# A float64 rounding's last addition on VectorE, a folded matrix two roundings behind, and token sums apart from their read

## The chip, the cores and the metric

The kernel runs on one core of a Trainium2 chip. A core has five engines with a queue each, which run in order: TensorE (PE, matmuls into PSUM; PEld is its weight load), VectorE (DVE), ScalarE (ACT), GpSimd (POOL) and SyncE (SP, which here only issues transfers). ACT and POOL issue transfers too, between their other instructions. Instructions on different engines wait for each other through semaphores. The metric is the device time of one execution in microseconds (us).

## The reference

Eight sequences of 3008 tokens with 256 channels pass a filter in the frequency domain and then an MLP mixer. All tokens' data are float32, the mixer's weights are float64.

```python
X = np.fft.rfft(x, axis=1)
y = np.fft.irfft(X * (filt_r + 1j * filt_i)[None], n=3008, axis=1)   # (8, 3008, 256)
h = np.maximum(y.transpose(0, 2, 1) @ w_tok1, 0.0) @ w_tok2          # (3008, 256), (256, 3008)
u = y + h.transpose(0, 2, 1)
out = u + np.maximum(u @ w_ch1, 0.0) @ w_ch2                         # (256, 1536), (1536, 256)
```

## The kernel before

**The filter.** 3008 = 47 x 64, so the Fourier transform is made of matmuls with small matrices. For each sequence 12 units (`a_unit`) transform x over the 64 and write the result to `z_tmp` in DRAM; x is loaded by SP into three tiles used in turn, the load for unit i + 3 issued behind unit i. Then come 32 frequency steps. `b_unit` reads its rows of `z_tmp` back, transforms over the 47 (PE), and multiplies by the filter (four DVE instructions, lines 378 to 381); `bi_unit` transforms back over the 47 and writes to `g_tmp`. The filter is loaded for two steps at a time into three tiles used in turn; for the first sequence SP, ACT and POOL issue these loads, for the others SP alone. `dft(bs)` is a generator that yields between units and steps: 12 units, 2 empty yields, 33 steps for the first sequence.

**The inverse over the 64** is not made for itself. It is a matrix `wai`. For the tokens it is multiplied into `w_tok1` beforehand: `w1_fold(i)` (line 241) multiplies two of the 24 slices of `w1` by it on PE, into the PSUM bank `po0` or `po1`, and ACT copies the result over the slices (line 246).

**The weights** arrive as float64 and are rounded to float32 on the chip (`rounded`, line 203): POOL issues the load into a staging tile, ACT takes the top bits (line 217), four DVE instructions (218, 219, 221, 223) build a truncated number `top` and the `rest`, and POOL adds the two into the weight (line 225). `top` and `rest` of the early weights lie in one tile `both`, of which there are two. `weights()` yields after each rounding, and each call of `next(convert)` makes one and then issues the load six ahead. The order: 12 tiles of `w1`, 16 of `w2`, 2 of `wc1`, and 10 late ones of `wc1` and `wc2`, of which those of `wc2` are followed by five more POOL instructions (lines 289 to 293) that form sums for a fast matrix product.

**The order of the work** is written by hand: each engine's queue is in the order of the program. The first sequence's transform runs first, with the 12 roundings of `w1` between its units (every second) and its steps (every third, up to step 15), each followed at once by its fold. Then SP issues the loads of the result (`t4_load`), the 16 roundings of `w2` follow, then `token_hidden(0)`: the token matmuls (line 423) into the bank `acc` and the ReLU on ACT (line 426). Two roundings of `wc1` and the first mixer tiles (`u_unit`: lines 437, 442, 444) come next. From there `mix` runs over six token tiles of six hidden pairs for each sequence, with the ten late roundings in its first half items and the next sequences' transforms spread among its items. `hidden` (449, 451), `sums` (464 to 466) and `products` (480) form an item, and POOL issues the stores of the output.

Of the kernel before, what the change touches and what calls it, by code (L numbers as in the profile page):

```python
# [14 lines left out]
ALU = mybir.AluOpType  # L15
# [5 lines left out]
N2 = 64  # L21
# [4 lines left out]
A = 24  # L26
# [9 lines left out]
TC = DT // P  # L36
# [7 lines left out]
NG = 8  # L44
# [69 lines left out]
def kernel(  # L114
# [11 lines left out]
    nc = tc.nc  # L126
# [33 lines left out]
    def bank(tag):  # L160
        return (psg if tag == "pg" else psum).tile([P, 512], FP32, tag=tag, name="ps_" + tag)
# [41 lines left out]
    def rounded(st, n, parts, late=False):  # L203

        words = [st.bitcast(t).rearrange("p (n w) -> p n w", w=2)[:, 0:n] for t in (U32, FP32)]
        lo, hi, hi_f = words[0][:, :, 0], words[0][:, :, 1], words[1][:, :, 1]
        if late:

            top = pp.tile([P, 512], FP32, tag="p1", name="top")[:, 0:n]
            rest = pp.tile([P, 512], FP32, tag="p2", name="rest")[:, 0:n]  # L210
        else:
            both = hp.tile([P, 2, 512], FP32, tag="hh", name="both")
            top, rest = both[:, 0, 0:n], both[:, 1, 0:n]
        top_i, rest_i = top.bitcast(U32), rest.bitcast(U32)


        nc.scalar.activation(out=top, in_=hi_f, func=AF.Copy, scale=2.0 ** -112)  # L217
        nc.vector.tensor_scalar(out=top_i, in0=top_i, scalar1=3, scalar2=None, op0=ALU.logical_shift_left)
        nc.vector.scalar_tensor_tensor(out=top_i, in0=hi, scalar=0x80000000, in1=top_i,  # L219
                                       op0=ALU.bitwise_and, op1=ALU.bitwise_or)  # L220
        nc.vector.tensor_scalar(out=rest_i, in0=top_i, scalar1=0xFF800000, scalar2=None, op0=ALU.bitwise_and)  # L221

        nc.vector.scalar_tensor_tensor(out=rest, in0=lo, scalar=2.0 ** -52, in1=rest, op0=ALU.mult, op1=ALU.mult)  # L223
        for src, dst in parts:
            nc.gpsimd.tensor_tensor(out=dst, in0=src(top), in1=src(rest), op=ALU.add)  # L225

    def w1_load(i):
        st = stage(512)
# [12 lines left out]
    def w1_fold(i):  # L241

        ps = bank("po%d" % (i % 2))
        w = w1[:, 2 * i:2 * i + 2, :].rearrange("p a t -> p (a t)")
        nc.tensor.matmul(ps, wai_t, w, start=True, stop=True)
        nc.scalar.copy(out=w, in_=ps)
# [169 lines left out]
        t4[b, c] = t4p.tile([P, TC4, D], FP32, tag="t4", name="t4")  # L416
        nc.sync.dma_start(t4[b, c], rows_of(g_d, b)[:, ts(c, TC4), :])

    def token_hidden(b):
        acc = bank("acc").rearrange("p (t d) -> p t d", t=TC)  # L420
        for a in range(A):
            for t in range(TC):
                nc.tensor.matmul(acc[:, t, :], w1[:, a, ts(t, P)], t4[b, a // TC4][:, a % TC4, :],  # L423
                                 start=(a == 0 and t == 0), stop=(a == A - 1 and t == TC - 1))
        h1 = h1p.tile([P, TC, D], FP32, tag="h1", name="h1")
        nc.scalar.activation(out=h1, in_=acc, func=AF.Relu)  # L426
        return h1

    def width(m):
        return 512 if m < MT - 1 else 448  # L430
# [15 lines left out]
    def hidden(ut, jt, w, hh):  # L446
        ps = bank("pg")
        for c in range(DH):
            nc.tensor.matmul(ps[:, 0:w], wc1[:, c, ts(jt, P)], ut[:, c, 0:w],  # L449
                             start=(c == 0), stop=(c == DH - 1))  # L450
        nc.scalar.activation(out=hh[:, jt % 2, 0:w], in_=ps[:, 0:w], func=AF.Relu)  # L451
# [8 lines left out]
    def sums(hh, w):  # L460
        hw = w // 2
        t = tp.tile([P, 4, 256], FP32, tag="t", name="t")
        v = nc.vector.tensor_tensor
        v(out=t[:, 0:2, 0:hw], in0=hh[:, :, hw:w], in1=hh[:, 0, 0:w].rearrange("p (s n) -> p s n", s=2), op=ALU.subtract)  # L464
        v(out=t[:, 2, 0:hw], in0=t[:, 1, 0:hw], in1=hh[:, 0, 0:hw], op=ALU.add)  # L465
        v(out=t[:, 3, 0:hw], in0=t[:, 2, 0:hw], in1=hh[:, 1, 0:hw], op=ALU.subtract)  # L466
        return t

    def products(m, jp, hh, t, po):
        w = width(m)  # L470
        hw = w // 2
        if jp == 0:
            for i in range(4):
                po.append(bank("po%d" % i).rearrange("p (s n) -> p s n", s=2))
        b11, b21, b22 = hh[:, 0, 0:hw], hh[:, 1, 0:hw], hh[:, 1, hw:w]
        t1, t3, t2, t4_ = (t[:, i, 0:hw] for i in range(4))
        todo = ((1, b21), (2, b22)), ((3, t4_), (6, t1)), ((0, b11), (5, t2)), ((4, t3),)
        for i, parts in enumerate(todo):
            for j, (n, mov) in enumerate(parts):
                nc.tensor.matmul(po[i][:, j, 0:hw], wc2[:, jp, n, :], mov, start=(jp == 0 and j == 0),  # L480
                                 stop=(jp == JP - 1 and j == len(parts) - 1))
# [35 lines left out]
    h1s, uts = {}, {}  # L517

    def u_part(b, m, dh):
        if dh == 0:  # L520
            uts[b, m] = up.tile([P, DH, 512], FP32, tag="u", name="u")
        u_unit(b, m, h1s[b], uts[b, m], dh)

    def mix(b, next_ready, convert):

        wait = [0]
        pos, hhs, sms = {}, {}, {}
        more = b + 1 < B

        items = [(m, jp) for m in range(MT) for jp in range(JP)]  # L530
        n = len(items)
        for i in range(n + 1):
            for half in range(2):
                next(convert, None)
                if i < n:
                    m, jp = items[i]
                    if half == 0:
                        hhs[i] = hp.tile([P, 2, 512], FP32, tag="hh", name="hh")
                    hidden(uts[b, m], 2 * jp + half, width(m), hhs[i])
                    if half == 1:  # L540
                        sms[i] = sums(hhs[i], width(m))
                        if m + 1 < MT and jp in (2, 3):
                            u_part(b, m + 1, jp - 2)
                            if jp == 3:
                                wait.append(m + 1)
                        if more and i == n - 2:
                            h1s[b + 1] = token_hidden(b + 1)
                        if more and i == n - 1:
                            u_part(b + 1, 0, 0)
                elif more and half == 0:  # L550
                    u_part(b + 1, 0, 1)
                if half == 1 and i >= 1:
                    m, jp = items[i - 1]
                    products(m, jp, hhs.pop(i - 1), sms.pop(i - 1), pos.setdefault(m, []))
                    if jp == JP - 1:
                        finish(b, m, uts[b, m], pos[m])
                if more and next_ready():
                    for c in wait:
                        t4_load(b + 1, c)
                    wait.clear()  # L560
                yield

    with tc.manual_schedule():
        nc.sync.dma_start(wa, wa_d)
        nc.vector.memset(xlast[HALF:P, XC - 1, :], 0.0)
        for t in filts:
            nc.vector.memset(t, 0.0)
        convert = weights()
        next(convert)
        folds = iter(range(A // 2))  # L570
        for i, _ in enumerate(dft(GROUPS[0])):
            if i == 0:
                for t, src in ((wai_t, wait_d), (wai, wai_d)):
                    nc.scalar.dma_start(t, src)

            if i % 2 == 1 and i < NXC or i % 3 == 2 and NXC < i <= NXC + 3 * (A // 4):
                next(convert)
                w1_fold(next(folds))
        assert next(folds, None) is None
        for c in range(A // TC4):  # L580
            t4_load(0, c)
        for _ in range(TC * N2 // NG):
            next(convert)
        h1s[0] = token_hidden(0)
        for _ in range(DH):
            next(convert)
        for dh in range(DH):
            u_part(0, 0, dh)
        for bs, after in zip(GROUPS, GROUPS[1:] + ((),)):
            todo = dft(after) if after else iter(())  # L590
            done = not after
            for b in bs:
                def next_ready():
                    return b != bs[-1] or done

                for i, _ in enumerate(mix(b, next_ready, convert)):
                    if not done and i % len(bs) == 0:
                        done = next(todo, "end") == "end"
            for _ in todo:
                raise AssertionError("the filter's steps don't fit beside the mixer's")  # L600
# [30 lines left out]
```

## Time and profile before

| | |
|---|---|
| median of 3 runs | 2754.22 us (2753.38 to 2755.7) |
| the profiled execution | 2754.93 us, its span 2753.2 us |
| instructions | 26044 |
| PE busy | 2603.7 us, 95% of the span |
| DVE busy | 1214.5 us, 44% |
| ACT busy | 528.6 us, 19% |
| POOL busy | 558.1 us, 20% |

A row of the timeline has the start and the length in us, engine, line, operation, the tile written and those read, shapes, the number of instructions that it merges, and in brackets how long the engine had been idle and what ended that. `ACTq`, `SPq` are the queues' own instructions, among them the issues of transfers. In a table by stage each engine has its busy time and its instructions in brackets; the last three columns are PE's granted clock (1.00 is full), the mean busy share of the 16 DMA engines and the GB/s that they moved. A row of the waits names who waited for whom, the total, the times and the longest. In a table of groups stand the busy time, the mean length of one in ns, and the idle time before them. The view of transfers has packets, bytes and the mean rate.

### The profile page before, as it was taken

The numbers are of one execution on the slowest core, as the hardware profiler recorded it, in microseconds if no ns is written. First come the engines' busy times: TensorE is split into PE (matmuls) and PEld (weight loads), VectorE is DVE, ScalarE is ACT, GpSimd is POOL, SyncE is SP. The second block draws the span as 40 slices with busy tenths as digits, with TensorE's granted clock in tenths as the row PEclk, the third lists the DMA queues.
The fourth block names the chain that finished last, engine by engine and source line by source line (L and its number), as shares of the span: only waits on it lengthen the run. The fifth ranks groups of instructions, "written<-read, shape, count | busy, mean of one in ns | idle before, by whom it ended". The sixth has DMA issues, their size and how long they took to land.

```text
span 2753.2 us, 26044 instructions
## 1 busy us (share of the span) xinstructions
PE 2603.7 (95%) x9112; PEld 1677.2 (61%) x9112; DVE 1214.5 (44%) x2244; ACT 528.6 (19%) x941; POOL 558.1 (20%) x973
## 2 busy tenths in 40 slices
PE   4466999999999999999999999999999999999997
PEld 1234655576666665676666765676666766676665
DVE  2478557723235455423325455432345443323333
ACT  1112222212222122112221112111212111111111
POOL 2338411112112111211212111121121121212121
PEclk8668999999999999999999999999999999999999
DMA  6455444323232222212223222211322111000000
GB/s 173 134 180 163 130 129 119 92 79 102 73 103 73 63 82 68 73 27 68 84 90 87 73 75 81 71 35 53 96 62 75 53 45 48 23 8 15 8 16 15
DMA packets 166488, 209.40 MB, mean 76 GB/s; under 512 B 35740, under 2 KB 114993, under 8 KB 166358
## 3 DMA queue, kind: packets, MB, share of 16 engines
q1 hardware_dynamic: 92297, 111.04, 13.8%
q0 software_dynamic: 30976, 44.53, 6.4%
q10 hardware_dynamic: 43085, 52.17, 5.8%
q8 instruction: 73, 1.20, 0.2%
q14 instruction: 57, 0.47, 0.1%
HBM read 132.63 MB, written 74.97 MB: 75 GB/s over the span
## 4 chain that ended last, share of the span: by engine, by line
PE 90%; DVE 4%; issue 2%; DMA 2%; POOL 1%; ACT 0%; SPq 0%; ACTq 0%; DVEq 0%; POOLq 0%
PE ps_pg L449 35%; PE ps_po L480 31%; PE ps_acc L437 6%; PE ps_acc L423 5%; PE ps_acc L386 4%; PE ps_b L370 4%; PE ps_acc L442 3%; PE ps_b L338 2%; DVE both L219 1%; POOL w L225 1%; DMA filt<-in_filt_r_dram 1%; DVE both L223 0%; DMA filt<-in_filt_i_dram 0%; DMA x<-in_x_dram 0%; DVE both L221 0%
## 5 line engine op out<-in xcount | busy, mean ns | idle before, releaser
L449 PE MATMUL ps_pg<-u,wc 128*128 128x512 f32 (+1 forms) x2304 | 1044.4, 583 | 0.0
L515 POOL DMA_DIRECT2D out_dram<-r x757 | 409.8, 550 | 2028.8 <-DVE r L505 2008.0
L449 PEld LDWEIGHTS ps_pg<-u,wc 128*128 128x128 f32 x2304 | 437.3, 190 | 418.7 <-issue 404.6
L451 ACT ACTIVATE hh<-ps_pg 128x512 f32<-128x512 f32 (+1 forms) x576 | 338.8, 588 | 1465.8 <-PE ps_pg L449 1463.6
L464 DVE TENSOR_TENSOR t<-hh 128x512 f32<-128x512 f32 (+1 forms) x288 | 196.6, 683 | 944.6 <-ACT hh L451 943.5
L480 PE MATMUL ps_po<-t,wc 128*128 128x256 f32 (+1 forms) x2304 | 581.2, 375 | 0.3 <-DVE t L466 0.3
L480 PEld LDWEIGHTS ps_po<-t,wc 128*128 128x128 f32 x2304 | 437.4, 190 | 50.2 <-DVE t L466 0.7
L480 PE MATMUL ps_po<-hh,wc 128*128 128x256 f32 (+1 forms) x1728 | 460.6, 375 | 0.7 <-POOL wc L293 0.7
L480 PEld LDWEIGHTS ps_po<-hh,wc 128*128 128x128 f32 x1728 | 321.2, 190 | 112.7 <-issue 83.3
L378 DVE TENSOR_TENSOR p<-ps_b,filt 128x512 f32<-128x512 f32 (+1 forms) x144 | 86.0, 598 | 392.3 <-PE ps_b L370 379.8
L437 PE MATMUL ps_acc<-w,h 128*128 128x512 f32 (+1 forms) x384 | 180.0, 591 | 22.8 <-ACT h L426 16.7
L423 PE MATMUL ps_acc<-t,w 128*128 128x256 f32 x768 | 170.0, 384 | 7.0 <-DMA t<-g_tmp 7.0
L423 PEld LDWEIGHTS ps_acc<-t,w 128*128 128x128 f32 x768 | 147.8, 193 | 30.6 <-ACT both L217 7.7
L386 PE MATMUL ps_acc<-p,wi 128*96 128x512 f32 (+1 forms) x320 | 147.3, 544 | 10.7 <-DVE p L381 4.3
L370 PE MATMUL ps_b<-t,wb 96*128 96x512 f32 (+1 forms) x288 | 132.9, 544 | 8.1 <-DVE p L380 5.5
L437 PEld LDWEIGHTS ps_acc<-w,h 128*128 128x128 f32 x384 | 73.1, 191 | 109.6 <-issue 101.7
L442 PEld LDWEIGHTS ps_acc<-wai,t 128*128 128x128 f32 x768 | 102.6, 194 | 45.2 <-issue 45.2
L466 DVE TENSOR_TENSOR t<-t,hh 128x256 f32<-128x256 f32 (+1 forms) x288 | 123.8, 430 | 9.9
L391 ACT COPY t<-ps_acc 96x512 f32<-96x512 f32 (+1 forms) x160 | 79.5, 497 | 252.2 <-PE ps_acc L386 228.4
L465 DVE TENSOR_TENSOR t<-t,hh 128x256 f32<-128x256 f32 (+1 forms) x288 | 122.4, 425 | 9.8
L490 DVE TENSOR_TENSOR u<-ps_po,u 128x256 f32<-128x256 f32 (+3 forms) x240 | 113.0, 517 | 8.6 <-PE ps_po L480 1.4
L442 PE MATMUL ps_acc<-wai,t 128*128 128x128 f32 (+1 forms) x768 | 101.9, 276 | 0.0
(59 smaller groups left out, 1169.8 us busy)
## 6 DMA issues: line engine op xcount, KB each, us to landing
z_tmp<-t ACTq DMA_DIRECT2D x96, 256.0 KB
t<-z_tmp SPq DMA_DIRECT2D x128, 192.0 KB
g_tmp<-t ACTq DMA_DIRECT2D x128, 192.0 KB
t<-g_tmp SPq DMA_DIRECT2D x48, 512.0 KB
x<-in_x_dram SPq DMA_DIRECT2D x176, 128.0 KB
out_dram<-r POOLq DMA_DIRECT2D x698, 32.0 KB, 1.8
wb<-wb_t SPq DMA_DIRECT2D x80, 96.0 KB
wi<-wi_t SPq DMA_DIRECT2D x80, 96.0 KB
```

The source lines that it names most:

```text
L370: nc.tensor.matmul(ps, wbs[k // WC][:, k % WC, :], t2s[k // KC][:, k % KC], start=True, stop=True)
L386: nc.tensor.matmul(ps[0:KR], wis[k // WC][:, k % WC, :], prods.pop(k), start=True, stop=True)
L423: nc.tensor.matmul(acc[:, t, :], w1[:, a, ts(t, P)], t4[b, a // TC4][:, a % TC4, :], start=(a == 0 and t == 0), stop=(a == A - 1 and t == ...
L437: nc.tensor.matmul(ps[:, 0:w], h1[:, t, ts(dh, P)], w2[:, t, ds(m * 512, w)], start=(t == 0), stop=False)
L442: nc.tensor.matmul(ps[:, ds(q * P, n)], t4[b, c][:, r, ts(dh, P)], wai[:, 0:n], start=False, stop=(q == 3))
L449: nc.tensor.matmul(ps[:, 0:w], wc1[:, c, ts(jt, P)], ut[:, c, 0:w], start=(c == 0), stop=(c == DH - 1))
L451: nc.scalar.activation(out=hh[:, jt % 2, 0:w], in_=ps[:, 0:w], func=AF.Relu)
L464: v(out=t[:, 0:2, 0:hw], in0=hh[:, :, hw:w], in1=hh[:, 0, 0:w].rearrange("p (s n) -> p s n", s=2), op=ALU.subtract)
L465: v(out=t[:, 2, 0:hw], in0=t[:, 1, 0:hw], in1=hh[:, 0, 0:hw], op=ALU.add)
L466: v(out=t[:, 3, 0:hw], in0=t[:, 2, 0:hw], in1=hh[:, 1, 0:hw], op=ALU.subtract)
L480: nc.tensor.matmul(po[i][:, j, 0:hw], wc2[:, jp, n, :], mov, start=(jp == 0 and j == 0), stop=(jp == JP - 1 and j == len(parts) - 1))
L515: q.dma_start(rows[g, e, :, ds(h * A + 4 * m, n)], blocks[ts(g, CW), h, e, 0:n])
```

## The change

In `rounded` the addition goes from POOL to DVE, for all 40 roundings. The folds no longer follow their own rounding: after the third and each later rounding of `w1` the tile rounded two before is folded, and the last two folds stand behind the first two roundings of `w2`. `token_hidden` is split: `token_sums`, the matmuls, is called behind the third rounding of `w2` for the first sequence, and `token_relu`, the read by ACT, stays behind the sixteenth. For the other sequences both are called where `token_hidden` was.

```diff
         for src, dst in parts:
-            nc.gpsimd.tensor_tensor(out=dst, in0=src(top), in1=src(rest), op=ALU.add)
+            nc.vector.tensor_tensor(out=dst, in0=src(top), in1=src(rest), op=ALU.add)
...
-    def token_hidden(b):
+    def token_sums(b):
         acc = bank("acc").rearrange("p (t d) -> p t d", t=TC)
...
+        return acc
+
+    def token_relu(acc):
         h1 = h1p.tile([P, TC, D], FP32, tag="h1", name="h1")
...
-                            h1s[b + 1] = token_hidden(b + 1)
+                            h1s[b + 1] = token_relu(token_sums(b + 1))
...
-        folds = iter(range(A // 2))
+        folds = []
...
                 next(convert)
-                w1_fold(next(folds))
-        assert next(folds, None) is None
+                folds.append(len(folds))
+                if len(folds) > 2:
+                    w1_fold(len(folds) - 3)
         for c in range(A // TC4):
             t4_load(0, c)
-        for _ in range(TC * N2 // NG):
+        for i in range(TC * N2 // NG):
             next(convert)
-        h1s[0] = token_hidden(0)
+            if i < 2:
+                w1_fold(A // 2 - 2 + i)
+            if i == 2:
+                acc = token_sums(0)
+        h1s[0] = token_relu(acc)
```

## The prediction

> **What bounds the kernel now.** The busy time of each engine by stage was read first; the stages are cut where the page's slices and the waits change.
>
> ```profile
> core 0: us, PE busy (x) PEld busy (x) DVE busy (x) ACT busy (x) POOL busy (x), PEclk, DMA share, GB/s
> 0.00:30.00 30.00, 9.55 (x10) 2.85 (x10) 5.25 (x8) 5.46 (x8) 8.82 (x19) 1.00 0.81 208
> 30.00:72.00 42.00, 19.99 (x24) 7.36 (x24) 8.96 (x16) 9.21 (x17) 9.08 (x12) 0.67 0.47 143
> 72.00:84.00 12.00, 2.93 (x4) 1.18 (x4) 2.41 (x5) 1.11 (x2) 7.98 (x14) 0.55 0.65 166
> 84.00:156.00 72.00, 35.03 (x74) 18.54 (x75) 39.71 (x88) 12.50 (x27) 23.84 (x37) 0.64 0.44 125
> 156.00:191.00 35.00, 26.11 (x66) 13.75 (x64) 26.59 (x64) 6.48 (x19) 8.11 (x15) 0.70 0.57 161
> 191.00:249.00 58.00, 29.47 (x108) 23.07 (x108) 55.52 (x73) 11.03 (x20) 49.55 (x65) 0.69 0.63 195
> 249.00:300.00 51.00, 49.46 (x156) 28.71 (x157) 42.10 (x59) 17.15 (x29) 36.39 (x48) 0.97 0.52 156
> 300.00:2753.00 2453.00, 2431.14 (x8673) 1581.75 (x8672) 1033.95 (x1934) 465.68 (x823) 414.36 (x766) 1.00 0.23 66
> ```
>
> From 300 us on PE is busy 2431.1 of 2453.0 us: nothing else counts there, and the change adds no matmul and takes none away. The case is decided before 250 us, where PE is busy about half the time, and what is saved there comes off the end one for one. Up to 191 us no engine is full, DVE, ACT and POOL least of all, and the transfers are at half their share: the engines wait for one another. The table of waits (0 to 300 us) says for whom:
>
> ```profile
> POOL w L225 <- DVE both L223: 100.7, 24, 15.9
> ...
> PE ps_po L245 <- POOL w L225: 65.3, 11, 10.7
> ```
>
> The timeline shows one round of the first stage (two forward units and one rounding) as a closed loop:
>
> ```profile
> 61.45 0.66 ACT L217 ACTIVATE both<-st 128x512 f32<-128x512 f32 x1 [0.48 <-ACT t L340]
> ...
> 62.21 0.43 DVE L218 TENSOR_SCALAR both<-both 128x512 uint32<-128x512 uint32 x1 [8.08 <-ACT both L217]
> ...
> 64.64 1.25 POOL L225 TENSOR_TENSOR w<-both 128x512 f32<-128x512 f32 x1 [8.15 <-DVE both L223]
> ...
> 65.95 2.07 PE L245 MATMUL ps_po<-w,wai_t 128*128 128x512 f32 x2 [5.60 <-POOL w L225]
> ...
> 67.82 1.92 PE L338 MATMUL ps_acc<-x,wa 128*128 128x512 f32 x2
> ...
> 68.06 0.59 ACT L246 COPY w<-ps_po 128x512 f32<-128x512 f32 x1 [5.95 <-PE ps_po L245]
> ...
> 71.42 0.33 ACTq L341 DMA_DIRECT2D z_tmp<-t  x1
> 71.87 0.66 ACT L217 ACTIVATE both<-st 128x512 f32<-128x512 f32 x1 [0.48 <-ACT t L340]
> ```
>
> L217 on ACT, four operations on DVE, the add on POOL, the fold on PE, the two units queued behind the fold, their copies on ACT, and then the next L217: 71.87 - 61.45 = 10.42 us a round, in which each engine waits for the one before it. In the third stage (191 to 249) it is DVE that is full, 55.5 of 58.0 us.
>
> **Part 1, folds two roundings late: first stage.** The fold now finds its tile two rounds old, so PE passes it and the units behind it wait for their x alone. Nothing is removed or added, 12 folds and 12 copies stay. A round's work is 20.0 us of PE in the four rounds from 30 to 72, so 5.0 each; DVE 8.96 / 4 = 2.2 plus the add; ACT 2.3 and its issues. All are half of 10.42. What is late next is data:
>
> ```profile
> DMA packets 6068, 12.23 MB, mean 170 GB/s; under 512 B 1036, under 2 KB 1755, under 8 KB 6067
> ```
>
> ```profile
> 10.00:20.00 10.00, 2.04 (x2) 0.50 (x2) 2.24 (x4) 1.48 (x3) 2.40 (x4) 1.00 1.05 275
> 15.00:25.00 10.00, 2.16 (x3) 1.15 (x4) 2.24 (x4) 0.73 (x2) 2.27 (x3) 1.00 0.95 261
> ```
>
> The first row is the view of transfers up to 72 us, the others two stretches in which the DMA engines are full, at 268 GB/s in the mean. 12.23 MB at that rate take 45.6 us; with some 3 us before transfers flow, 49. I take 50 for the last issue of z_tmp, which stood at 71.42: **-21.4**. At most -24 (the last tiles of w1 can land later); at least -10, should the ring of three x tiles, refilled only after a unit has read one, not keep the queues full.
>
> **The crossing to the second stage.** The first product needs the filter, whose transfers ACT issues behind the copy of the fold, and POOL behind its add:
>
> ```profile
> 78.49 0.60 ACTq L183 DMA_DIRECT2D filt<-in_filt_r_dram  x1
> ```
>
> ```profile
> 83.83 0.42 DVE L378 TENSOR_TENSOR p<-ps_b,filt 128x256 f32<-128x256 f32 x1 [8.86 <-DMA filt<-in_filt_r_dram]
> ```
>
> It came 83.83 - 71.42 = 12.4 us after the last z_tmp issue. ACT's issue came 7.1 us after it, nearly all of it the rounding and the fold. In the new order ACT has only L217 (0.66) and a copy that is ready (0.59) ahead: some 1.7 us. Then 83.83 - 78.49 = 5.3 us as before make 7.0: **-5.4** (from -2 to -6.5; w1's last tiles are still under way then).
>
> **Second stage, 32 frequency steps with six roundings among the first 16.** The second half has no rounding:
>
> ```profile
> 156.48 0.42 DVE L378 TENSOR_TENSOR p<-ps_b,filt 128x256 f32<-128x256 f32 x1 [4.36 <-PE ps_b L370]
> ```
>
> ```profile
> 188.48 0.43 DVE L381 TENSOR_TENSOR p<-p,p 128x256 f32<-128x256 f32 x1
> ```
>
> (188.91 - 156.48) / 16 = 2.03 us a step. The first half takes (156.48 - 83.83) = 72.65 us, 40 more than 16 x 2.03 = 32.5: 6.7 us a rounding, though it occupies DVE for 64.64 - 62.21 = 2.4 us. With the fold out of the way DVE carries 2.4 and the add (0.69 for 512 elements, a row below), so 3.1, and I give it 0.4 for the wait for L217: 3.5. 32 x 2.03 + 6 x 3.5 = 86.0 against 188.91 - 83.83 = 105.1: **-19.1**. The matmuls of a fold (2.07) lie beside the rounding. POOL's filter loads are no longer queued behind an add. Half of it, -9, if the filter loads and z reads, already waited for in the second half, stretch the steps; -28 if steps fall to DVE's own four operations (4 x 0.43 = 1.75).
>
> **Part 2, the add on DVE: third stage, 16 roundings of w2 and two of wc1.** DVE is the path:
>
> ```profile
> 191.63 0.35 DVE L218 TENSOR_SCALAR both<-both 128x376 uint32<-128x376 uint32 x1 [2.72 <-ACT both L217]
> 192.02 0.55 DVE L219 SCALAR_TENSOR_TENSOR both<-st,both 128x376 uint32<-128x376 uint32 x1
> ...
> 193.46 0.35 DVE L218 TENSOR_SCALAR both<-both 128x376 uint32<-128x376 uint32 x1
> 193.84 1.71 DVE L219 SCALAR_TENSOR_TENSOR both<-st,both 128x376 uint32<-128x376 uint32 x1
> ...
> 248.72 0.68 DVE L444 COPY u<-ps_acc 128x512 f32<-128x512 f32 x1
> ```
>
> ```profile
> L225 POOL TENSOR_TENSOR w<-both 128x368 f32<-128x368 f32 x16 | 24.3, 1518 | 21.2 <-DVE both L223 21.1
> ```
>
> The first rounding, with POOL idle, takes 193.46 - 191.63 = 1.83 us; the later ones 3.0 or more, since L219 lasts 1.71 while POOL adds (0.55 at 192.02, alone). The add on DVE has 368 elements and then 8. Rows with two operands in SBUF give 0.43 for 256 and 0.69 for 512, some 1.0 ns an element: 0.54 and 0.18. So 1.83 + 0.04 + 0.54 + 0.18 = 2.59 a rounding, 41.4 for 16; the two of 512 take 3.1 - 0.1 = 3.0 each. 47.4 against 248.72 - 191.63 = 57.1: **-9.7**. The strided store of w2 is not shown on DVE: at worst POOL's price of 1.52 and 0.53, 1.33 more, 16 x 1.33 = 21 us, so +12 for the stage; at best -11. I take the nearer rows, of the same engine.
>
> **Late roundings (249 to 300), ten beside a PE that is nearly full.** DVE takes 6 x 0.86 + 4 x 0.69 = 7.9 us more, on 42.1 of 51.0; POOL sheds the adds of the row below, which now stretch L219 and the others.
>
> ```profile
> L225 POOL TENSOR_TENSOR wc<-top,rest 128x256 f32<-128x256 f32 x12 | 10.3, 878 | 11.6 <-DVE rest L223 11.6
> ```
>
> I take **0**, from -1 to +5 (DVE late for the products).
>
> **Part 3, token sums and their read.**
>
> ```profile
> 197.18 23.78 PE L423 MATMUL ps_acc<-t,w 128*128 128x256 f32 x96 [6.98 <-DMA t<-g_tmp]
> ```
>
> On PE the sums follow the last two folds, with no other PE work among the 16 roundings; the read stays behind the 16th L217 on ACT, as now. Between the t4 loads and that L217 lie over 30 us (16 x 2.59 less some 6 until t4 has landed, 197.18 - 191) for 23.8 us of matmuls: 0. The two folds moved here cost about 4 us of PE, under the wait for t4.
>
> **Sum.** -21.4 - 5.4 - 19.1 - 9.7 = -55.6. The profiled execution took 2754.9 (span 2753.2 and 1.7 around it): 2699.3. The median shown, 2754.2, is 0.7 lower; I say **2699**.
>
> **The rivals.** *Data hold the loops.* The ring of x, the filter loads and, in the third stage, w2 behind the loads of t4 leave about half: -10 - 3 - 9 - 6 = -28, so 2727. For: full shares up to 25 us. Against: shares of 0.44 to 0.47 between 30 and 156.
>
> *The fold still waits for the newest add*, if w1 were watched as one tile. Then PE keeps its wait, a round loses only 1.25 - 0.69, 12 x 0.6 = 7 us, and the third stage gives its 9.7: 2738. Against it, w2 is one tile as well:
>
> ```profile
> 237.71 2.04 PE L437 MATMUL ps_acc<-w,h 128*128 128x512 f32 x2 [16.75 <-ACT h L426]
> 243.91 2.08 PE L437 MATMUL ps_acc<-w,h 128*128 128x512 f32 x2 [4.15 <-POOL w L225]
> ```
>
> The first half of w2 was read at 237.71 while adds to the second half went on until 243.9.
>
> *Faster still:* steps at 1.75 us (-9) and x by 47 (-3): 2687.
>
> *The slower one: DVE's add is held by POOL's descriptors.* POOL issues the next load just as DVE comes to the add.
>
> ```profile
> 225.62 1.99 POOL L271 DMA_DIRECT2D st<-in_moe_w_ch_dram  x4
> ...
> 226.88 2.65 DVE L219 SCALAR_TENSOR_TENSOR both<-st,both 128x376 uint32<-128x376 uint32 x1
> ```
>
> ```profile
> 248.11 0.69 DVE L223 SCALAR_TENSOR_TENSOR both<-st,both 128x512 f32<-128x512 uint32 x1
> ```
>
> ```profile
> 247.01 2.12 POOL L271 DMA_DIRECT2D st<-in_moe_w_ch_dram  x4
> ```
>
> L219 begun at 226.88 didn't end before POOL's issues and the add behind them: 2.65 - 0.55 = 2.1 us held. For 40 roundings that is 84: 2783. It decides from 55.6 / 40 = 1.4 us a rounding on. Against it: L223 at 248.11 ran its 0.69 under four such issues. The Trainium skill (SBUF — State Buffer, "Who interferes with whom") says that a DVE instruction with two SBUF inputs contends with a GpSimd instruction that reads SBUF. By that the issues cost the add nothing, and only POOL's sums of wc2 can hold it; the trace agrees in the 1.71 of L219 beside an add and the 0.69 beside issues.
>
> **How the numbers follow.** Forecast 0.56, data 0.24, fold still waits 0.07, faster still 0.08, slower 0.03; 0.02 for data and part of the holding together, near no change. The range leaves out the fold's case, the slower ones and the tails: 2682 to 2732. About 0.2% (5.5 us) is what can be told from no change: faster 0.95, same 0.02, slower 0.03.
>
> **What would show it.** Right: no wait of L245 for an add; the last z_tmp issue near 50; the first L378 near 57; rounding periods of 9 to 10 us in the second stage; the last step near 143; L219 at 0.55 throughout, and 2.6 us a rounding of w2; PE full from about 195 on. Wrong: a DMA share below 0.6 before 50 us with PE waiting for x; an add on DVE well over 0.54; PE waiting at L480 after the start-up.

## The result, and the profile after

| | before | changed | ratio, 95% interval |
|---|---|---|---|
| median, 4 runs each | 2753.8 us | 2692.99 us (2691.02 to 2694.39) | 0.9778 [0.9761, 0.9794] |
| profiled execution, span | 2753.2 us | 2689.2 us | |

The forecast was 2699 us in a range of 2682 to 2732. The busy time by stage of the changed kernel, cut where its own waits change (the columns are those of the table before):

```profile
15.00:30.00 15.00, 9.76 (x13) 2.69 (x12) 6.97 (x13) 5.19 (x9) 2.19 (x4) 1.00 1.03 327
30.00:44.00 14.00, 9.27 (x16) 3.28 (x16) 6.24 (x11) 4.67 (x9) 2.05 (x4) 0.88 0.91 272
44.00:53.00 9.00, 1.74 (x3) 1.17 (x4) 4.90 (x9) 1.48 (x3) 7.43 (x14) 0.71 0.83 227
53.00:104.00 51.00, 33.41 (x78) 19.10 (x76) 44.01 (x95) 12.52 (x27) 16.70 (x29) 0.72 0.68 188
104.00:134.00 30.00, 23.02 (x59) 12.72 (x60) 25.59 (x63) 5.89 (x16) 8.13 (x15) 0.70 0.62 179
134.00:187.00 53.00, 32.73 (x115) 24.32 (x113) 48.38 (x107) 12.53 (x23) 17.23 (x32) 0.75 0.72 220
187.00:238.00 51.00, 51.00 (x161) 29.41 (x162) 41.35 (x74) 18.52 (x31) 22.39 (x38) 0.97 0.52 159
238.00:2689.00 2451.00, 2429.22 (x8669) 1580.95 (x8667) 1033.27 (x1933) 464.49 (x821) 411.67 (x758) 1.00 0.22 66
```

The last row is the old one from 300 us on, 62 us earlier and with nearly the same busy time (2429.2 us of PE where there were 2431.1): what was saved lies ahead of it. In the first two rows the transfers stand at 1.03 and 0.91, where the old stage from 30 to 72 us had 0.47. The first half of the second stage, from 53 to 104 us, has DVE at 44.0 of 51.0 us, where it had 39.7 of 72.0 (from 84 to 156).

The timeline of the changed kernel shows the opened loop:

```profile
41.67 0.67 ACT L217 ACTIVATE both<-st 128x512 f32<-128x512 f32 x1 [2.36 <-DMA z_tmp<-t]
...
42.28 1.02 PE L245 MATMUL ps_po<-w,wai_t 128*128 128x512 f32 x2
...
44.37 0.33 ACTq L341 DMA_DIRECT2D z_tmp<-t  x1
44.75 0.69 DVE L225 TENSOR_TENSOR w<-both 128x512 f32<-128x512 f32 x1
44.82 0.67 ACT L217 ACTIVATE both<-st 128x512 f32<-128x512 f32 x1 [0.48 <-DVE both L223]
44.87 0.60 ACTq L183 DMA_DIRECT2D filt<-in_filt_r_dram  x1
```

This L245 stands in the program behind the sixth rounding, the one whose L217 is at 44.82 and whose add comes at 47.99. It folds the fourth tile, whose add began at 39.47, and has no bracket: it waited for nothing. In the waits from 0 to 300 us L245 has no row at all, where it had 65.3 us before. With the fold only one rounding behind, it would have needed the add at 44.75, 2.5 us later. The next L217 follows after 3.15 us here; the five rounds from the first L217 (19.94) to that one (44.82) take 4.98 us in the mean, where the round shown of the old kernel took 10.42. ACT's filter loads are issued 0.5 us after the last z_tmp instead of 7.1. The third stage:

```profile
138.74 0.35 DVE L218 TENSOR_SCALAR both<-both 128x376 uint32<-128x376 uint32 x1
...
139.13 0.55 DVE L219 SCALAR_TENSOR_TENSOR both<-st,both 128x376 uint32<-128x376 uint32 x1
...
140.69 0.86 DVE L225 TENSOR_TENSOR w<-both 128x368 f32<-128x368 f32 x2
141.24 0.69 POOL L253 DMA_DIRECT2D st<-in_moe_w_tok_dram  x1 [2.03 <-DVE both L223]
141.46 0.35 DVE L218 TENSOR_SCALAR both<-both 128x376 uint32<-128x376 uint32 x1
```

L219 is at 0.55, the 1.71 are gone. A rounding takes 141.46 - 138.74 = 2.72 us here. The stages by their marks in the timelines (starts of instructions in us; the last hidden column is the first matmul of `hidden`):

| kernel | last z_tmp | first L378 | last L381 | first L218 of w2 | first tile u copied | first hidden | span |
|---|---|---|---|---|---|---|---|
| before | 71.42 | 83.83 | 188.48 | 191.63 | 248.72 | 253.56 | 2753.2 |
| changed | 44.37 | 52.49 | 132.94 | 136.02 | 186.19 | 191.31 | 2689.2 |
| add alone (first run) | 70.39 | 79.81 | 180.20 | 182.78 | 233.08 | 237.95 | 2735.8 |
| folds alone (second) | 43.38 | 51.97 | 134.97 | 137.61 | 194.64 | 199.77 | 2697.7 |
| sums at the end (third) | 44.87 | 53.22 | 133.72 | 136.31 | 186.51 | 191.46 | 2692.5 |
| lag of one (fourth) | 44.01 | 52.53 | 135.18 | 137.76 | 187.98 | 192.90 | 2694.1 |
| four x tiles (fifth) | 42.22 | 51.11 | 135.11 | 137.69 | 187.86 | 192.98 | 2690.9 |
| late adds on POOL (sixth) | 45.80 | 53.25 | 134.58 | 137.16 | 187.39 | 192.48 | 2693.9 |
| long runs (seventh) | 43.85 | 51.82 | 133.02 | 136.10 | 184.39 | 190.41 | 2690.1 |
| flat store (eighth) | 45.42 | 53.57 | 135.63 | 138.71 | 188.92 | 194.47 | 2692.4 |
| three ahead (ninth) | 44.74 | 50.50 | 135.46 | 138.54 | 188.72 | 193.84 | 2691.8 |
| flat on both sides (tenth) | 45.00 | 53.15 | 132.90 | 135.48 | 181.20 | 187.22 | 2688.3 |
| three ahead, long runs (eleventh) | 44.58 | 50.14 | 133.37 | 135.96 | 184.28 | 190.11 | 2721.5 |
| ring of three (twelfth) | 38.77 | 49.88 | 135.12 | 138.20 | 188.39 | 193.52 | 2691.4 |

The 2721.5 us are those of an execution with a lower granted clock, 0.95 from 500 to 1000 us where the changed kernel has 1.00.

Six of these kernels are the same program up to the last L381: the changed one and the third, sixth, seventh, eighth and tenth run. Their last z_tmp lies between 43.85 and 45.80, their first L378 between 51.82 and 53.57, their last L381 between 132.90 and 135.63, so a difference of this size between two traces shows nothing. The third stage (first L218 of w2 to the first tile u) is steadier: 50.17 to 50.30 us in the eight kernels that share the changed kernel's rounding of w2. From the first hidden matmul to the end all but the eleventh take 2497.9 to 2501.4 us, in no order that goes with the changes.

### The profile page after: what moved, and what is told of

It is laid out like the page before. It is cut to its first block, busy times and chain, and to the rows that moved or that the text cites. A ratio compares the mean times of both kernels' runs of the same rounds, so it can differ in the third digit from the quotient of the medians.

```text
span 2689.2 us, 26030 instructions
## 1 busy us (share of the span) xinstructions
PE 2594.6 (96%) x9112; PEld 1675.0 (62%) x9112; DVE 1213.7 (45%) x2306; ACT 527.8 (20%) x941; POOL 495.4 (18%) x911
## 4 chain that ended last, share of the span: by engine, by line
PE 93%; DVE 3%; DMA 2%; issue 1%; POOL 0%; ACT 0%; SPq 0%; ACTq 0%; DVEq 0%; POOLq 0%
PE ps_pg L452 36%; PE ps_po L483 31%; PE ps_acc L440 6%; PE ps_acc L423 5%; PE ps_acc L386 4%; PE ps_b L370 4%; PE ps_acc L445 3%; PE ps_b L338 3%; DMA x<-in_x_dram 1%; DVE both L219 0%; DVE both L223 0%; DVE p L380 0%; DVE p L379 0%; DMA t<-z_tmp 0%; DMA filt<-in_filt_r_dram 0%
## 5 line engine op out<-in xcount | busy, mean ns | idle before, releaser
L378 DVE TENSOR_TENSOR p<-ps_b,filt 128x512 f32<-128x512 f32 (+1 forms) x144 | 86.0, 597 | 371.0 <-PE ps_b L370 370.3
L386 PEld LDWEIGHTS ps_acc<-p,wi 128*96 128x96 f32 x320 | 53.3, 175 | 88.7 <-issue 65.3
```

The source lines that it names most:

```text
L386: nc.tensor.matmul(ps[0:KR], wis[k // WC][:, k % WC, :], prods.pop(k), start=True, stop=True)
```

## The experiments

**Each part alone.** First the add without the late folds:

```diff
-                if len(folds) > 2:
-                    w1_fold(len(folds) - 3)
+                w1_fold(len(folds) - 1)
...
-            if i < 2:
-                w1_fold(A // 2 - 2 + i)
-            if i == 2:
-                acc = token_sums(0)
-        h1s[0] = token_relu(acc)
+        h1s[0] = token_relu(token_sums(0))
```

> The changed kernel with each fold put back right behind its own rounding and the token sums put back behind the sixteenth rounding of w2; only the add stays on VectorE. Theory (the late folds open the loops of the first two stages, the add frees only the shared port in the third): the round of the first stage stays a closed loop and gets shorter by the add's 1.25 - 0.69 us, 12 x 0.6 = 7 us for both stages; the third stage keeps its 7 us and the late part its 2 us: 2754 - 16 = 2738 us, last issue of z_tmp near 68 us. Rival (PE waited for POOL's queue with its transfers, not for the order of the folds): most of the 61 us stays, 2700 us, last issue of z_tmp near 46.

Measured: 2736.67 us, ratio 0.9939 [0.9922, 0.9955] to before. The timeline and the waits of this kernel (0 to 200 us; who waited for whom, total, times, longest):

```profile
60.59 0.66 ACT L217 ACTIVATE both<-st 128x512 f32<-128x512 f32 x1 [0.46 <-ACT t L340]
...
64.40 2.07 PE L245 MATMUL ps_po<-w,wai_t 128*128 128x512 f32 x2 [4.89 <-DVE w L225]
...
70.82 0.66 ACT L217 ACTIVATE both<-st 128x512 f32<-128x512 f32 x1 [0.46 <-ACT t L340]
```

```profile
PE ps_po L245 <- DVE w L225: 52.4, 10, 8.3
```

The loop is closed as before, 10.23 us instead of 10.42 at this place; only the engine for which PE waits has another name. The last z_tmp comes at 70.39. What POOL's queue held was not the matter. The third stage, 233.08 - 182.78 = 50.3 us, is that of the changed kernel.

Then the folds without the add:

```diff
-            nc.vector.tensor_tensor(out=dst, in0=src(top), in1=src(rest), op=ALU.add)
+            nc.gpsimd.tensor_tensor(out=dst, in0=src(top), in1=src(rest), op=ALU.add)
```

> The changed kernel with the add put back on POOL; folds and token sums stay late. Theory: the first stage is bound by transfers as in the changed kernel (last issue of z_tmp 44 to 46), the second within 3 us of it, and the third stage takes its 57 us again with L219 near 1.7 us: 2693 + 7 + 2 = 2702 us. Rival (both parts are needed for the loops, since POOL's add then holds its transfer issues): 2715 us or more.

Measured: 2700.85 us, 0.9803 [0.9789, 0.9818]. The group of L219 in its third stage (mean of one in ns behind the busy time):

```profile
L219 DVE SCALAR_TENSOR_TENSOR both<-st,both 128x376 uint32<-128x376 uint32 x16 | 29.2, 1822 | 0.6
```

The first two stages end at 134.97, within the 132.90 to 135.63 of the six with the same start, and the third takes 57.03 us, as before the change. In spans the folds alone save 55.5 us, the add alone 17.4, both 64.0; up to the first hidden matmul it is 53.8, 15.6 and 62.3. The parts add up to 7 us more than both, since part of what the add gives alone is a shorter closed loop (8 us up to the last L381), and the late folds open that loop anyway.

**The place of the token sums, and the lag.**

```diff
-            if i == 2:
-                acc = token_sums(0)
-        h1s[0] = token_relu(acc)
+        h1s[0] = token_relu(token_sums(0))
```

> The changed kernel with the token sums issued behind the sixteenth rounding of w2, next to their read. Theory: TensorE's order of instructions is the same, so the time is: 2693 us, first token matmul near 142 us as in the changed kernel. Rival (the place in the program moves the wait of the first token matmul or of the bank): the sums begin near 175 us and the time is 15 us or more longer.

Measured: 2694.4 us, 0.978 [0.9765, 0.9794]; the two rows are the first token matmuls of this kernel and of the changed one:

```profile
142.10 22.85 PE L423 MATMUL ps_acc<-t,w 128*128 128x256 f32 x96 [5.45 <-DMA t<-g_tmp]
```

```profile
141.68 23.45 PE L423 MATMUL ps_acc<-t,w 128*128 128x256 f32 x96 [4.33 <-DMA t<-g_tmp]
```

Both wait for the loads of t4. The third part of the change does nothing measurable.

```diff
-                if len(folds) > 2:
-                    w1_fold(len(folds) - 3)
+                if len(folds) > 1:
+                    w1_fold(len(folds) - 2)
...
-            if i < 2:
-                w1_fold(A // 2 - 2 + i)
+            if i < 1:
+                w1_fold(A // 2 - 1)
```

> The changed kernel with each fold one rounding behind its tile instead of two. Theory: a tile rounded one round (6 us or more) ago is finished when the fold comes, so nothing changes: 2693 us. Rival (TensorE comes to the fold so early that a lag of one still waits): waits of L245 for the add of 1 us or more a round, 2700 us or more.

Measured: 2694.63 us, 0.9781 [0.9767, 0.9796]. In time the theory holds, in its reason not quite: the waits of this kernel (0 to 140 us) show that with a lag of one PE does wait for adds of the first stage,

```profile
PE ps_po L245 <- DVE w L225: 6.5, 3, 2.4
```

three times, 2.4 us at most. The last z_tmp is at 44.01 all the same, so these waits lay beside others, presumably those for x.

**What binds the first stage.**

```diff
-    xp = pool("xp", 3)
+    xp = pool("xp", 4)
...
-        for u in todo[0:3]:
+        for u in todo[0:4]:
...
-            if i + 3 < len(todo):
-                x_load(*todo[i + 3])
+            if i + 4 < len(todo):
+                x_load(*todo[i + 4])
```

> The changed kernel with four x tiles in turn instead of three, loaded four ahead. Theory (transfers bind the first stage: their engines are busy 0.91 to 1.03 of it): the last issue of z_tmp stays within 2 us of 44.4 and the time within 3 us of 2693. Rival (the ring of three, refilled only when a unit has read one, binds): the stage gets shorter by up to a quarter, the last issue of z_tmp near 35 to 38, the time 2685 us or less.

Measured: 2695.32 us, 0.9787 [0.9772, 0.9802]; the last z_tmp at 42.22. That is 2.2 us sooner than in the changed kernel and 1.6 sooner than in any of the six with the same start; the transfers stopped it there. Its busy time by stage:

```profile
15.00:30.00 15.00, 11.70 (x15) 3.59 (x14) 6.30 (x11) 5.29 (x9) 2.04 (x4) 1.00 1.05 309
30.00:42.30 12.30, 7.09 (x15) 2.02 (x13) 8.37 (x14) 5.70 (x10) 2.96 (x6) 1.00 1.05 330
```

The share is 1.05 to the end of the stage. At the last L381 (135.11) nothing of this is left.

Fewer bytes, then. A first try lowered the number of loads ahead:

```diff
-        load(AHEAD)
+        load(AHEAD // 2)
...
-            load(i != n - 1)
+            load(2 if A // 2 - AHEAD // 2 <= i < A // 2 else i != n - 1)
```

> The changed kernel with the weights loaded three roundings ahead at first instead of six, and two loads a step at the last three roundings of w1, so that six are ahead again for w2. Until the crossing 3 x 0.52 = 1.57 MB of w1 less are moved. Theory (transfers bind the first stage, at 270 to 330 GB/s): the last issue of z_tmp and the first product come 5 us sooner, near 39 and 47, and what is moved later is hidden in the second stage, where DVE binds: 2688 us. Rival (the latency of the x loads binds, or the transfers put off are missed at once in the second stage): 2692 us or more.

Measured: 2693.52 us, 0.9778 [0.9764, 0.9791]; the last z_tmp at 44.74. The view of transfers up to 15 us has this row in the changed kernel, and its like in this one:

```profile
st<-in_moe_w_tok_dram POOLq DMA_DIRECT2D x14, 256.0 KB, 10.4
```

```profile
st<-in_moe_w_tok_dram POOLq DMA_DIRECT2D x14, 256.0 KB, 10.9
```

So this run did not do what it was made for: with the add gone from its queue, POOL has nothing to wait for and issues loads until the staging tiles run out (seven, two transfers each). The number ahead no longer sets the pace of the first loads, and the stage isn't shorter. But POOL comes to its first filter load at 30.31 instead of 46.32, and the first product comes at 50.50, 1.3 us or more ahead of the six kernels with the same start; at the last L381 (135.46) that is gone. The same with the seventh run's add (below):

> Loads three ahead at first as in the ninth run, together with w2's add in 16 runs of 23 as in the seventh, whose third stage was 48.3 us instead of 50.2. If both add up: 1.9 us below the ninth run, 2686 us by the theory of transfers; 2690 us or more if the loads put off are missed.

Measured: 2692.72 us, 0.9777 [0.9763, 0.979], the median of six of which one, the one in the table, took 2723.32. The first product comes at 50.14 and the last L381 at 133.37, again without a gain; the third stage, 48.3 us, is that of the seventh run. The last run makes the ring of staging tiles three:

```diff
-    stages = [(t4p, "t4")] * (A // 2) + early * 3 + late * 2
+    stages = (early[0:3]) * (A // 6) + early * 3 + late * 2
...
-        load(AHEAD)
+        load(AHEAD // 2)
...
-            load(i != n - 1)
+            load(1 + AHEAD // 2 if i == A // 2 - 1 else i != n - 1)
```

> The changed kernel with w1's staging tiles in a ring of three instead of seven, so that POOL can't run ahead: three loads ahead at first (the ninth run's number alone changed nothing, 14 loads of w1 were issued by 15 us in both), and four loads at the last rounding of w1, so that six are ahead for w2. About 1 MB of w1 less is moved before 44 us. Theory (transfers bind the first stage, at 270 to 330 GB/s): the last issue of z_tmp comes 3 to 5 us sooner, near 40, and the first product near 48; the second stage, bound by DVE, hides what was put off: 2689 us. Rivals: the latency of x binds (z_tmp stays near 44), or the transfers put off are missed in the second stage (z_tmp near 40, but the last product at 133 as before): 2692 us or more.

Measured: 2696.23 us, 0.9793 [0.978, 0.9807]. The views of transfers up to 44.7 us, first the changed kernel, then this one:

```profile
DMA packets 5986, 12.09 MB, mean 270 GB/s; under 512 B 1022, under 2 KB 1741, under 8 KB 5986
```

```profile
DMA packets 5932, 11.34 MB, mean 254 GB/s; under 512 B 1010, under 2 KB 1773, under 8 KB 5931
```

The last z_tmp is issued at 38.77, 5.6 us sooner than in the changed kernel and 5.1 sooner than in any of the six with the same start: transfers bind the first stage, as the theory has it. But then the waits of this kernel (5 to 60 us) show

```profile
PE ps_b L370 <- DMA wi<-wi_t: 9.9, 1, 9.9
```

and the first product comes 2.6 us sooner only. From there to the last L381 it takes 85.2 us, where the six kernels with the same start take 79.8 to 82.1, so that the last L381, at 135.12, is no sooner than theirs. DVE's waits at L378 (49 to 136 us), without the first, come to 8.2 us, 2.6 of them for the filter and 2.3 for wi, where the changed kernel has 4.4, with 0.3 for the filter. The outcome is that of the second rival: what is put off is missed at once. In all runs with late folds the last L381 lies between 132.9 and 135.6, whatever the last z_tmp (38.8 to 45.8) and the first product (49.9 to 53.6) do. That up to there data are the common bound, besides DVE, fits shares of 0.62 to 1.03, but it wasn't tested by itself.

**The late adds.**

```diff
-            nc.vector.tensor_tensor(out=dst, in0=src(top), in1=src(rest), op=ALU.add)
+            (nc.gpsimd if late else nc.vector).tensor_tensor(out=dst, in0=src(top), in1=src(rest), op=ALU.add)
```

> The changed kernel with the adds of the ten late roundings (wc1 and wc2 beside the mixer) put back on POOL. Theory: there DVE's extra 8 us and POOL's port hold cancel, only the 1.1 us that TensorE waited at L480 come back: 2694 us. Rival (the late adds on DVE delay the sums for the products, a cost hidden in the total): 2689 us or less.

Measured: 2695.09 us, 0.9785 [0.9769, 0.9801]. PE's waits from 188 to 310 us:

```profile
PE ps_acc L440 <- DVE u L447: 3.1, 1, 3.1
PE ps_po L483 <- POOL wc L293: 0.7, 1, 0.7
PE ps_po L483 <- DVE t L469: 0.5, 1, 0.5
```

The first wait, for the first tile u, the changed kernel has too (2.9 us, ended at 186.93, ahead of this stretch); apart from it PE waits for nothing there. By the waits, the other 1.2 us are what the late adds on DVE save; in the time alone they can't be told from noise.

**The price of the strided add.** It was 0.79 us, where the forecast had 0.54 (the groups follow below).

```diff
-            return bass.AP(tensor=v.tensor, offset=v.offset, ap=[v.ap[0], [A, 2], [1, w], [N1, NG]])
+            return bass.AP(tensor=v.tensor, offset=v.offset, ap=[v.ap[0], [N1, NG], [A, 2], [1, w]])
...
-        rounded(st, n, [(both, dst[:, :, :, ds(g * NG, NG)]), ...
+        rounded(st, n, [(both, dst[:, :, :, ds(g * NG, NG)].rearrange("p h a n -> p n h a")), ...
```

> The changed kernel with the add of w2 walking its 368 elements in 16 runs of 23 (source contiguous, store 512 bytes apart) instead of 46 runs of 8 (source 188 bytes apart, store contiguous). The add took 0.79 us where the rows gave 0.54. Theory (a price for each short run, 0.25 us / 46): 0.63 us, 16 x 0.16 = 2.6 us less in the third stage, 2690 us. Rival (it is the distance of the elements, not the runs): 0.79 us or more, 2693 us or more.

Measured: 2693.58 us, 0.9781 [0.9766, 0.9796]; third stage 48.29 us. Then a contiguous store:

```diff
-        rounded(st, n, [(both, dst[:, :, :, ds(g * NG, NG)]), ...
+        rounded(st, n, [(both, w2[:, t, ds(g * 2 * w * NG, 2 * w * NG)].rearrange("p (h a n) -> p h a n", h=2, a=w)), ...
```

> The changed kernel with the add of w2 storing its 368 elements in one contiguous piece; it leaves out the permutation of w2, and the source is still read 188 bytes apart in runs of 8. Theory (the runs of the store cost the 0.25 us): 0.54 us an add, 16 x 0.25 = 4 us less, 2689 us. Rival (the strided read costs it): 0.79 us, 2693 us.

Measured: 2693.83 us, 0.9779 [0.9765, 0.9794]; third stage 50.21 us. Last, both sides contiguous:

```diff
         def both(v):
-            return bass.AP(tensor=v.tensor, offset=v.offset, ap=[v.ap[0], [A, 2], [1, w], [N1, NG]])
+            return v[:, 0:2 * w * NG]
...
-        rounded(st, n, [(both, dst[:, :, :, ds(g * NG, NG)]), ...
+        rounded(st, n, [(both, w2[:, t, ds(g * 2 * w * NG, 2 * w * NG)]), ...
```

> The changed kernel with w2's large add reading and storing 368 elements in one contiguous piece; it leaves out the permutation of w2. Theory (the broken pattern of either side costs the add its 0.25 us): 0.54 us an add, the third stage 3 to 4 us shorter than 50.2. Rival (0.79 us comes from something else, as the 368 elements or the small add behind): 0.79 us again.

Measured in one run: 2690.36 us; third stage 45.72 us. The group of the large add (busy time, mean of one in ns), for the changed kernel and for the seventh, eighth and tenth runs:

```profile
L225 DVE TENSOR_TENSOR w<-both 128x368 f32<-128x368 f32 x16 | 12.7, 792 | 0.5
```

```profile
L225 DVE TENSOR_TENSOR w<-both 128x368 f32<-128x368 f32 x16 | 12.7, 791 | 0.5
```

```profile
L225 DVE TENSOR_TENSOR w<-both 128x368 f32<-128x368 f32 x16 | 12.7, 793 | 0.6
```

```profile
L225 DVE TENSOR_TENSOR w<-both 128x368 f32<-128x368 f32 x16 | 8.7, 542 | 0.6
```

The contiguous add takes what the forecast had. With source elements 188 bytes apart, in 46 groups of 8, the add takes 0.25 us more, with a whole store (eighth run) as with a broken one (changed kernel): a whole store doesn't help while the source is broken like this. In the seventh run, whose source has 16 runs of 23, it is the same 0.25 us, where the theory of a price for each run had an add of 0.63 us; but there the store goes 512 bytes apart, and no whole source with a broken store was tried, so which side costs it there is not shown. The seventh run's stage is also 1.9 us shorter at the same recorded length of the add, since the small add behind it and the next L218 begin sooner. Nor is it any broken pattern: the adds of wc2, whose source goes in runs of 32, take in the changed kernel

```profile
L225 DVE TENSOR_TENSOR wc<-top,rest 128x256 f32<-128x256 f32 x12 | 5.0, 454 | 0.2
```

that is 0.45 us for 256 elements, 0.42 to 0.43 being the whole ones' price. Which property costs the 0.25 us stays open. Of the variants that keep the permutation of w2, none is faster than the changed kernel by more than their runs differ.

## Why the prediction was right, and where its terms were off

| step | forecast | measured, from the marks above |
|---|---|---|
| first stage, to the last z_tmp | -21.4 | -27.1 |
| crossing, to the first product | -5.4 | -4.3 |
| second stage, to the last L381 | -19.1 | -24.2 |
| third stage, w2 and wc1 | -9.7 | -6.9 |
| all else | 0 | -1.5 |
| sum (spans) | -55.6 | -64.0 |

The mechanism held in every step but the crossing, which came to its time by another path. The sizes were off by more than the sum shows, since they partly cancel: the first two stages and the rest gave 12.3 us more than forecast, the crossing and the third stage 3.9 less.

**First stage.** The mechanism is as told: the first run kept the loop with the add on DVE, the second opened it without. Transfers are late next: the twelfth run shows it. The size was off by the rate: 12.09 MB were moved by 44.7 us, about the 12.23 MB of the estimate, but from 15 to 44 us at 300 GB/s in the mean (327 and 272 in the rows), where the two old rows had given 268.

**Crossing.** ACT's issue came after 0.5 us, sooner than the 1.7 assumed, but the transfers then came through queues at a share of 0.83: 8.1 us instead of 7.0. The path was another, too. The forecast carried over the 5.3 us of the filter, while the first product now waited for PE, and PE for the read of z_tmp:

```profile
51.26 1.19 PE L370 MATMUL ps_b<-t,wb 96*128 96x256 f32 x2 [7.96 <-DMA t<-z_tmp]
```

```profile
52.49 0.42 DVE L378 TENSOR_TENSOR p<-ps_b,filt 128x256 f32<-128x256 f32 x1 [3.81 <-PE ps_b L370]
```

In the sixth, seventh and tenth runs, with the same start, the last wait of this L378 was again the filter, so the two come at nearly the same time.

**Second stage.** The rounding's price was right: the first half now takes 103.19 - 52.49 = 50.7 us (the 17th L378 starts at 103.19), the second 133.37 - 103.19 = 30.2, so 1.89 a step, and (50.7 - 16 x 1.89) / 6 = 3.4 us a rounding, where 3.5 were put in. The step itself was taken as unchanged at 2.03; 32 x 0.14 = 4.5 of the 5.1 us are that. In the old second half DVE waited 4.7 us at L378 (3.6 for the filter and, without the 4.36 that end at 156.48, 1.1 for PE), in the new one 2.7, all for PE: that is 2.0 of the 2.25 us between the two halves. Why the filter no longer comes late there is not settled.

**Third stage.** L219 is no longer held by POOL's add, as forecast: the second run has it at 1.82 us, the changed kernel at 0.55. The term that was too low is the add of w2, 0.54 put in and 0.79 measured, inside the bounds given (1.52 at worst), but taken from whole rows of another shape; an add well over 0.54 was one of the forecast's own signs of being wrong. The small add overlaps it, so that both take 0.86 us instead of 0.72, and L218 has a mean of 0.38 instead of 0.35. With 16 roundings at (180.24 - 136.02) / 16 = 2.76 us instead of 2.59 that is 2.8 us, the whole difference. The tenth run, with a whole pattern, has 45.7 us for the stage.

**Late roundings and token sums.** 0 and 0 held: the sixth run gives 1.2 us of waits to the late adds, the third no gain to the split. The -1.5 of all else is smaller than what the stretch behind the first hidden matmul differs between kernels (2497.9 to 2501.4 us).

**The rivals.** Data do hold the loops, but only after the gain was made. A fold that still waits did not occur with two behind; with one behind it does, three times, at no cost. The hold by POOL's descriptors did not occur: the L225 of 512 elements at 47.99 lies wholly beside POOL's issues of transfers, from 46.32 to 51.78, and takes 0.69 us. The Trainium skill (SBUF — State Buffer, "Who interferes with whom") says that a DVE instruction with two SBUF inputs contends only with a GpSimd instruction that reads SBUF; the second run (1.82) and the changed kernel (0.55) agree.

## What to carry to other kernels

Where a fast engine consumes at once what a chain of slower ones has just produced, and the chain's next turn is queued behind that consumer, put the consumer a turn or two later: it took nothing away and saved 54 of 2753 us here (second run, up to the first hidden matmul). Before counting further on such a gain, work out which resource is full once the loop is open; here it was the transfers, and the next 2 to 6 us won in the first stage were gone by the end of the second. Moving work to a busy engine can pay if it ends a hold between engines, but price it by the very access pattern that it has.

## What the hardware showed beyond that

With the add off its queue, POOL issued loads as far ahead as its tiles allowed. By 15 us it had issued 14 transfers of w1 with six loads ahead and with three, 6 with a ring of three tiles, and 12 in the two kernels with the add on POOL and six loads ahead: the ring of staging tiles set the pace, not the number.

The first DVE instruction of a rounding, L218, has a mean of 383 ns in the changed kernel's third stage and of 349 in the seventh and tenth runs, whose adds end sooner; beside it POOL issues the next load. The Trainium skill (SBUF — State Buffer, "Who interferes with whom") says that `tensor_scalar` in a two-port mode and GpSimd block each other. That fits only in part: eight of the sixteen take 0.39 to 0.43 us, but those at 141.46 and 174.80 take 0.35 although POOL issues beside them too (from 141.24 for 0.69 us, from 171.75 for 3.50). No run took the issue away, so the cause of these 0.03 us an instruction is not shown.
